# Second-layer weight sums taken in the attention loop, and splits of activations ordered later and joined in twos, in a fused attention and expert kernel

## The chip, the cores and the metric

The kernel runs on one core of a Trainium2 chip. The metric is the device time of one execution in microseconds. The engines have short names: PE is TensorE's matmuls and PEld its weight loads, DVE is VectorE, ACT is ScalarE, POOL is GpSimd, and SP issues most DMAs. PSUM has eight banks; every product of TensorE lands in one and has to be read out by DVE or ACT before the bank is used again.

## What is computed

Three layers follow each other: attention over keys and values that are averaged in eights, a mixture of experts in which every expert sees every token with a weight P from eight rounds of normalization, and a gated MLP. Cut to its core:

```python
# attention: q, k, v are (4, 8, 576, 64)
k_p = k.reshape(B, H, S // 8, 8, D).mean(axis=3)
v_p = v.reshape(B, H, S // 8, 8, D).mean(axis=3)
x = softmax(q @ k_p.T / sqrt(D)) @ v_p          # then laid out as (2304, 512)
# experts: w1 (8, 512, 1024), w2 (8, 1024, 512)
P = exp(x @ w_gate - max)
for _ in range(8):
    P /= P.sum(1, keepdims=True) + 1e-09
    P /= P.sum(0, keepdims=True) + 1e-09
    P *= N / E
out = sum(P[:, e:e+1] * (maximum(x @ w1[e], 0.0) @ w2[e]) for e in range(8))
# gated MLP: w_gate, w_val (512, 1536), w_out (1536, 512)
g = out @ w_gate
result = (g * sigmoid(g) * (out @ w_val)) @ w_out
```

## The kernel before

**Precision.** Every operand of a product is split into a high and a low part ("hi" and "lo", `split`): ACT copies the value to the rounded type (hi), and POOL or DVE subtracts hi from the value (lo). A product then is three matmuls (lines 114 to 116: hi·hi, hi·lo, lo·hi).

**Strassen products.** A 512-wide piece of a layer is worked as seven products M1 to M7 of half-size blocks instead of eight. Their operands are sums of blocks: on the weights' side `take_sums` (first layer, POOL, lines 695 to 698) and `row_sums` (second layer, DVE, lines 760 to 763), and on the activations' side a few sums too. The products of a piece share three PSUM banks, a, b and c; `part_sum` (line 985, ACT) copies an intermediate sum out of bank a, DVE adds it to what lies in another bank.

**Order.** Nothing is scheduled by a machine: each engine executes its instructions in the order in which the program issues them, and an instruction that waits holds up all that its engine has behind it. The author steers by queues in the Python code: `tasks` (work hung on a product's name), `late` (work to be issued at the next point, by `later()`), `side` (steps taken one at a time by `pump`), `do` (work for a point of a pair).

**Stages.** The attention loop (`for i in range(2, n_att)`, 20 row tiles) runs from about 50 to 183 us. One round i issues the query copy `qT` (line 271), scores, exponential (line 293), the multiplication by the reciprocal sum on POOL (line 303), the averages of values on POOL (line 244), and the stores of the result to `x_d`: hi from SP (line 477), lo added to it by a DMA that POOL issues (line 478). Between them `fill()` and `unit()` put matmuls of the first expert piece ("group 0", banks `hps` and `yps`), which keep TensorE busy. The PSUM pool `h` has two banks, shared by `qps`, `hps` and `gps`.

Pass 1 (about 224 to 726 us) works 30 `quad`s on the first 768 tokens: seven products, and between them six tiles `yps` of the second layer of the quad before (`second_tile`, lines 1054 to 1056, read out by DVE in line 1298 or 1300). The pool `y` has four banks. Meanwhile the quad prepares weights: first-layer sums, the splits of the w2 rows (`split_rows`), the row sums on DVE at M6, their split at M4 (ACT line 65, POOL line 66), and stores of all of these to DRAM (`w1s_d`, `w2s_d`). In the first quads the eight normalization rounds of P run too (lines 802 to 816).

Passes 2 and 3 (726 to 1645 us) read these sets back. Here `expert_quad`s run in 30 pairs; a pair's results are weighted by P (`whole`: lines 1354 and 1357), split (`split_h`: ACT line 1188, POOL or DVE line 1189) and combined (`sum_h`, POOL line 1201), and the second layer of the pair before is worked as seven `block`s (bank `mbs`, line 1245), one each after the points in `at_block`. Up to about 1470 us `conv` steps (ACT line 903, DVE lines 904 to 920) convert the weights of the last layer, one step a `pump`. The tail (1645 to 2113 us) is the gated MLP.

## Time and profile before

| what | value |
|---|---|
| three runs | 2111.4, 2116.02, 2122.97 us (median 2116.02) |
| the profiled execution | 2114.75 us |
| its span, first to last instruction | 2113.0 us |
| mean granted TensorE clock | 0.982 of full speed |
| busy share of the span: PE, DVE, POOL, ACT | 95%, 79%, 64%, 40% |
| TensorE not busy, 50 to 185 us | 5.2 us |
| TensorE not busy, 227.6 to 317 us (first quads) | 22.4 us |
| TensorE not busy, 317 to 725.8 us | 4.4 us |
| TensorE not busy, 725.8 to 763 us (pair 0) | 5.3 us |
| TensorE not busy, 763 to 1470 us (pairs with conversion) | 36.6 us |
| TensorE not busy, 1644.6 to 2113 us (tail) | 17.2 us |

The shares are averages over stages with different limits. What counts is, in each stage, how long TensorE stands or runs slowly and which engine's result it then waits for.

### The profile page before, as it was taken

The page shows a single profiled execution, that of the slowest core. Times are in us where ns is not written, and L with a number is a line of the kernel's source. Part 1 is how long each engine was busy: PE and PEld are TensorE (multiplying, and loading weights), DVE is VectorE, ACT ScalarE, POOL GpSimd, SP SyncE. Part 2 cuts the span into 40 slices and gives each one's busy share as a digit, 9 for nine tenths or more (in the row PEclk, how much of TensorE's full clock was granted, in tenths as well). Part 3 has the DMA queues.
Part 4 walks back from the last instruction along what each step waited for, and adds up shares of the span by engine and source line. Part 5 has one row for each costly group of instructions (what it writes and reads, how often), then busy time and mean ns, then how long its engine had stood idle before and what let it go on. Part 6 is the DMA issues. An engine that isn't in the chain of part 4 may idle for free.

```text
span 2113.0 us, 30988 instructions
## 1 busy us (share of the span) xinstructions
PE 2008.7 (95%) x11079; PEld 1891.9 (90%) x11079; DVE 1664.4 (79%) x2299; ACT 840.7 (40%) x1641; POOL 1361.4 (64%) x1117
## 2 busy tenths in 40 slices
PE   7999779999999989999999989999999899999999
PEld 7899668899999889999998989999999889899898
DVE  7774688888888868989887988988666867867776
ACT  3443324444444433333333422333333454544543
POOL 4444558888888467877776767877656546444432
PEclk8999889999999999999999999999999999999999
DMA  6463548888888788888888888888788654544442
GB/s 160 108 134 94 185 180 323 299 303 302 308 296 314 291 264 309 313 313 290 308 298 282 282 284 302 300 316 296 264 258 264 210 199 150 174 165 140 150 153 87
DMA packets 225754, 510.67 MB, mean 242 GB/s; under 512 B 35296, under 2 KB 119872, under 8 KB 219456
## 3 DMA queue, kind: packets, MB, share of 16 engines
q1 hardware_dynamic: 220704, 492.96, 67.9%
q0 software_dynamic: 4896, 15.73, 2.7%
q8 instruction: 88, 1.44, 0.3%
q14 instruction: 66, 0.54, 0.1%
HBM read 357.58 MB, written 151.04 MB: 241 GB/s over the span
## 4 chain that ended last, share of the span: by engine, by line
PE 69%; DVE 17%; DMA 7%; issue 3%; ACT 2%; POOL 2%; SPq 0%; ACTq 0%; DVEq 0%; POOLq 0%
PE aps L114 6%; PE aps L116 6%; PE aps L115 6%; PE yps L1054 5%; PE yps L1056 5%; PE yps L1055 5%; PE mbs L114 4%; PE mbs L115 4%; PE mbs L116 4%; PE cps L114 4%; PE cps L116 3%; PE cps L115 3%; DVE AC L1245 2%; DVE LR L1189 2%; DMA craw<-in_moe_w_val_dram 2%
## 5 line engine op out<-in xcount | busy, mean ns | idle before, releaser
L1201 POOL TENSOR_TENSOR LF<-LF 128x384 f32<-128x384 f32 x240 | 281.6, 1174 | 230.2 <-DVE LF L1357 136.6
L1188 ACT ACTIVATE LR<-LF 128x384 fp32r<-128x384 f32 x420 | 209.7, 522 | 373.9 <-DVE LF L1357 253.9
L985 ACT COPY LF<-aps 128x384 f32<-128x384 f32 x378 | 178.8, 473 | 401.5 <-PE aps L116 401.2
L1189 POOL TENSOR_TENSOR LR<-LF,LR 128x384 fp32r<-128x384 f32 x240 | 291.8, 1239 | 29.0 <-ACT LR L1188 29.0
L114 PE MATMUL mbs<-LR 128*128 128x384 f32 x840 | 285.1, 339 | 3.7 <-DVE AC L1245 3.7
L115 PE MATMUL mbs<-LR 128*128 128x384 f32 x840 | 284.0, 338 | 0.0
L116 PE MATMUL mbs<-LR 128*128 128x384 f32 x840 | 283.5, 338 | 0.0
L1054 PE MATMUL yps<-LR 128*128 128x512 f32 x576 | 229.3, 398 | 10.5 <-DVE AC L1300 6.3
L1245 DVE TENSOR_TENSOR AC<-mbs,AC 128x768 f32<-128x768 f32 x196 | 186.2, 950 | 67.2 <-PE mbs L116 66.9
L1056 PE MATMUL yps<-LR 128*128 128x512 f32 x576 | 228.0, 396 | 0.5 <-DVE LR L1498 0.5
L1055 PE MATMUL yps<-LR 128*128 128x512 f32 x576 | 227.6, 395 | 0.0
L734 POOL TENSOR_TENSOR LR<-praw,LR 128x512 fp32r<-128x512 f32 (+1 forms) x130 | 134.6, 1055 | 142.3 <-ACT LR L728 142.3
L734 POOL TENSOR_TENSOR LR<-sums,LR 128x1024 fp32r<-128x1024 f32 x65 | 159.5, 2454 | 60.7 <-ACT LR L728 60.7
L114 PEld LDWEIGHTS mbs<-LR 128*128 128x128 f32 x840 | 158.9, 189 | 5.5 <-DVE AC L1245 5.5
L115 PEld LDWEIGHTS mbs<-LR 128*128 128x128 f32 x840 | 159.0, 189 | 0.0
L116 PEld LDWEIGHTS mbs<-LR 128*128 128x128 f32 x840 | 158.8, 189 | 0.0
L1075 DVE SCALAR_TENSOR_TENSOR LR<-LF,LR 128x384 fp32r<-128x384 f32 x90 | 101.8, 1131 | 54.7 <-ACT LR L1074 54.7
L1189 DVE TENSOR_TENSOR LR<-LF,LR 128x384 fp32r<-128x384 f32 x180 | 136.8, 780 | 8.7 <-ACT LR L1188 8.7
L1357 DVE SCALAR_TENSOR_TENSOR LF<-LF,LR 128x384 f32<-128x384 f32 x180 | 135.6, 753 | 6.2
L1054 PEld LDWEIGHTS yps<-LR 128*128 128x128 f32 x576 | 110.1, 191 | 31.4 <-DVE AC L1300 8.5
L66 POOL TENSOR_TENSOR LR<-rraw,LR 128x512 fp32r<-128x512 f32 x72 | 114.0, 1603 | 30.4 <-ACT LR L65 29.1
L1056 PEld LDWEIGHTS yps<-LR 128*128 128x128 f32 x576 | 110.0, 191 | 25.2 <-DVE LR L1498 1.0
(284 smaller groups left out, 5662.8 us busy)
## 6 DMA issues: line engine op xcount, KB each, us to landing
LR<-w1s_d SPq DMA_DIRECT2D x210, 512.0 KB, 5.8
LR<-w2s_d SPq DMA_DIRECT2D x210, 512.0 KB, 5.3
w1s_d<-LR SPq DMA_DIRECT2D x29, 1792.0 KB, 8.5
w2s_d<-LR SPq DMA_DIRECT2D x30, 1024.0 KB, 4.2
w2s_d<-LR SPq DMA_DIRECT2D x90, 256.0 KB, 5.4
praw<-in_moe_w_dram SPq DMA_DIRECT2D x30, 512.0 KB, 6.0
rraw<-in_moe_w_dram SPq DMA_DIRECT2D x30, 512.0 KB, 5.0
LR<-rows_d POOLq DMA_DIRECT2D x12, 1024.0 KB, 7.2
```

Of the source, the lines that this page charges most:

```text
L114: nc.tensor.matmul(ps, lhsT=wh, rhs=ah, start=start, stop=False, skip_group_check=more)
L115: nc.tensor.matmul(ps, lhsT=wh, rhs=al, start=False, stop=False, skip_group_check=more)
L116: nc.tensor.matmul(ps, lhsT=wl, rhs=ah, start=False, stop=stop, skip_group_check=more)
L734: nc.gpsimd.tensor_tensor(out=lo, in0=src, in1=hi.bitcast(F32), op=ALU.subtract)
L985: nc.scalar.copy(out=t, in_=ps[:, :HB])
L1054: nc.tensor.matmul(ps, lhsT=hh[:, o:o + P], rhs=wh, start=j == 0, stop=False)
L1055: nc.tensor.matmul(ps, lhsT=hh[:, o:o + P], rhs=wl, start=False, stop=False)
L1056: nc.tensor.matmul(ps, lhsT=hl[:, o:o + P], rhs=wh, start=False, stop=j == 1)
L1188: nc.scalar.activation(out=hi, in_=src, func=AF.Copy)
L1189: f = lambda: eng.tensor_tensor(out=lo, in0=src, in1=hi.bitcast(F32), op=ALU.subtract)
L1201: nc.gpsimd.tensor_tensor(out=r(o), in0=r(a), in1=r(b), op=ALU.subtract)
L1245: nc.vector.tensor_tensor(out=acc_of(m), in0=ps[:, :, :HB], in1=acc_of(m), op=ALU.add)
```

## The change

**Early sums.** The row sums of the first 8 of 30 quads (`NEARLY`) are taken by a generator, `early_row_sums`, of which the attention loop runs four steps at the end of each round from i = 4 on. A set takes two rounds: load (SP), three sums (POOL), then the fourth sum (POOL), the hi copy (ACT), two halves of the lo part (POOL); the store is issued with the next load. For these eight quads pass 1 has no `row_sums` and no `split_row_sums` any more. In pass 1 the stores of the rows go from M7 to M3 and those of the row sums from M3 to M2 of the next quad.

**PSUM.** The pool `y` has three banks instead of four in pass 1, pair 0 and the tail, and c has two banks in turn there.

**Passes 2 and 3.** M4 now comes ahead of M3 in a quad. The weighing of the results 22 and 12 is one operation of 768 columns, several sums and splits are done two at a time, and they are issued at later points. The order of the blocks is now M1, M3, M2, M5, M7, M6, M4.

**Changes of pass.** The additions and stores of `combine` become single steps in `late`, or, after the last pass, in `side` during the tail; the fills of pair 0 are spread differently.

The diff, cut to its core:

```diff
+    def take_row_sums(eng, r, t):
+        a11, a12, a21, a22 = (r[:, k, c:c + 2 * P] for c in (0, 2 * P) for k in (0, 1))
+        for o, a, b, op in ((1, a21, a22, ALU.add), (2, t[:, 1], a11, ALU.subtract), (3, a11, a21, ALU.subtract),
+                            (0, a12, t[:, 2], ALU.subtract)):
+            yield lambda o=o, a=a, b=b, op=op: eng.tensor_tensor(out=t[:, o], in0=a, in1=b, op=op)
...
+    def early_row_sums():
+
+        t = AC[:, 6 * DM:8 * DM].rearrange("p (m f) -> p m f", m=4)
+        w = AC.bitcast(F32R)[:, 8 * DM:12 * DM].rearrange("p (m h f) -> p m h f", m=4, h=2)
+        for i in range(NEARLY):
+            r = rawp.tile([P, 2, DM], F32, tag="raw", name=f"early{i}")
+            nc.sync.dma_start(out=r, in_=rows[i].rearrange("(j p) d -> p j d", p=P))
+            yield
+            for f in take_row_sums(nc.gpsimd, r, t):
+                f()
+                yield
+            nc.scalar.activation(out=w[:, :, 0], in_=t, func=AF.Copy)
+            yield
+            for c in range(2):
+                m = slice(2 * c, 2 * c + 2)
+                nc.gpsimd.tensor_tensor(out=w[:, m, 1], in0=t[:, m], in1=w[:, m, 0].bitcast(F32), op=ALU.subtract)
+                yield
+            keep_row_sums(i, w)
...
             mask_values()
+            if i > 3:
+                for _ in range(4):
+                    next(early_sums, None)
...
-        pools["y"] = ps_open.enter_context(tc.tile_pool(name="ps_y2", bufs=4, **left))
+        pools["y"] = ps_open.enter_context(tc.tile_pool(name="ps_y2", bufs=3, **left))
+        banks_c = [ps_c, ps_open.enter_context(tc.tile_pool(name="ps_c2", bufs=1, **left))]
...
                 if expert:
+                    if n > NEARLY:
+                        at("M2", lambda: store_row_sums(n - 1))
                     at("M2", lambda: store_set(i))
-                    if n == 1:
-                        at("M2", lambda: split_row_sums(0))
-                        at("M5", lambda: store_row_sums(0))
-                    at("M6", lambda: row_sums(n))
-                    at("M4", lambda: split_row_sums(n))
-                    at("M3", lambda: store_row_sums(n))
+                    if n >= NEARLY:
+                        at("M6", lambda: row_sums(n))
+                        at("M4", lambda: split_row_sums(n))
                 at("M7", lambda: load_rows(n + 1))
-                at("M7", lambda: store_rows(n))
+                at("M3", lambda: store_rows(n))
...
             prod("M7")
             u3 = part_sum(banks["a"], "u3")
-            point("M7", lambda: whole("22", banks["c"], u3))
+            point("M7", lambda: csum("22", banks["c"], u3))
+            prod("M4")
+            point("M4", lambda: weigh("21", 1, banks["a"]))
             prod("M3")
-            point("M3", lambda: whole("12", banks["c"], u2))
-            prod("M4")
-            point("M4", lambda: whole("21", banks["a"], None))
+            point("M3", lambda: csum("12", banks["c"], u2), lambda: weigh("12", 2))
...
-            on(0, 0, lambda: split_h(0, "M1", r_of(0, "11")))
-            on(0, 2, lambda: split_h(0, "M3", r_of(0, "22"), V))
-            on(0, "M3", lambda: [sum_h(0, t) for t in ("T1", "T3", "T2")])
-            on(1, "M1", lambda: split_t(0, "T1"))
-            on(1, 3, lambda: split_h(1, "M1", r_of(1, "11")), lambda: split_t(0, "T2"))
-            on(1, 4, lambda: split_t(0, "T3"))
-            on(1, 5, lambda: split_h(0, "M2", r_of(0, "21"), V), lambda: split_h(1, "M3", r_of(1, "22"), V))
-            on(1, "M3", lambda: sum_h(0, "T4"), lambda: [sum_h(1, t) for t in ("T1", "T3", "T2")])
-            on(1, "M4", lambda: split_h(1, "M2", r_of(1, "21"), V))
-            on(1, 6, lambda: split_t(0, "T4"), lambda: sum_h(1, "T4"), lambda: split_t(1, "T1"))
+            on(0, 1, lambda: split_h(0, "M1", "11", 1, G))
+            on(0, "M3", lambda: sum_t13(0))
+            on(1, 3, lambda: split_h(0, "M3", "22", 2, V))
+            on(1, "M6", lambda: sum_t24(0))
+            on(1, 4, lambda: split_h(0, "M5", "11", 2, G), lambda: split_h(1, "M1", "11", 1, G))
+            on(1, "M3", lambda: sum_t13(1))
+            on(1, 6, lambda: split_h(1, "M3", "22", 2, V), lambda: split_h(0, "M6", "22", 2, V))
...
+            if j == NPR - 1:
+                rest.extend(combine(NPASS - 1, m))
+            elif last:
+                for f in combine(1 + j // (NQ // 2), m):
+                    late.append(f)
```

How the instructions stand on three engines, before and after. First ACT in round 7 of the attention loop; `e_110` holds the scores of tile 9, `kp` averaged keys, `AC` the buffer in which the early sums lie, `qT` the transposed queries, `hh` the hi part of group 0's activations, `aTh` that of the transposed attention weights. Before:

```order
L293 ACTIVATE e_110<-e_110 64x576
L220 COPY kp<-kp 128x5x64
L271 COPY qT<-qps 128x512
L135 ACTIVATE hh<-hps 128x256
L331 ACTIVATE aTh<-mps 128x5x128
```

After, with the line numbers of the changed program:

```order
L329 ACTIVATE e_110<-e_110 64x576
L256 COPY kp<-kp 128x5x64
L204 ACTIVATE AC<-AC 128x4x256
L307 COPY qT<-qps 128x512
L135 ACTIVATE hh<-hps 128x256
L367 ACTIVATE aTh<-mps 128x5x128
```

The copy of the early sums (L204) now stands between the key copy and the query copy. POOL in rounds 6 and 7: the multiplications of tiles 8 and 9 (`e_112`, `e_110`) and the averages of values (`kv`, `vp`). Before:

```order
L303 TENSOR_TENSOR e_112<-e_112,st 128x576
L244 TENSOR_TENSOR kv<-kv 128x256
L244 TENSOR_TENSOR kv<-kv 128x128
L244 TENSOR_TENSOR vp<-kv 128x64
L303 TENSOR_TENSOR e_110<-e_110,st 64x576
```

After:

```order
L339 TENSOR_TENSOR e_112<-e_112,st 128x576
L187 TENSOR_TENSOR AC<-early_920 128x256
L187 TENSOR_TENSOR AC<-AC,early_920 128x256
L187 TENSOR_TENSOR AC<-early_920 128x256
L280 TENSOR_TENSOR kv<-kv 128x256
L280 TENSOR_TENSOR kv<-kv 128x128
L280 TENSOR_TENSOR vp<-kv 128x64
L339 TENSOR_TENSOR e_110<-e_110,st 64x576
L187 TENSOR_TENSOR AC<-early_920,AC 128x256
L208 TENSOR_TENSOR AC<-AC 128x2x256 x2
```

Three sums of a set stand ahead of the averages, and the fourth, for which the copy on ACT waits, behind the multiplication. Last, DVE in the second half of a quad of passes 2 and 3, with steps of the conversion between: `cps` and `aps` are the banks c and a, `mbs` the bank of a second-layer block. Before:

```order
L1354 TENSOR_TENSOR LF<-cps,LF 128x384
L1357 SCALAR_TENSOR_TENSOR LF<-LF,LR 128x384
L908 TENSOR_SCALAR LF<-LF 128x512
L1245 TENSOR_TENSOR AC<-mbs,AC 128x768
L912 SCALAR_TENSOR_TENSOR LF<-craw,LF 128x512
L1189 TENSOR_TENSOR LR<-LF,LR 128x384
L1354 TENSOR_TENSOR LF<-cps,LF 128x384
L1357 SCALAR_TENSOR_TENSOR LF<-LF,LR 128x384
L1357 SCALAR_TENSOR_TENSOR LF<-aps,LR 128x384
L916 TENSOR_SCALAR LF<-LF 128x512
```

After:

```order
L1382 TENSOR_TENSOR LF<-cps,LF 128x384
L939 TENSOR_SCALAR LF<-LF 128x512
L1270 TENSOR_TENSOR AC<-mbs,AC 128x768
L943 SCALAR_TENSOR_TENSOR LF<-craw,LF 128x512
L1390 SCALAR_TENSOR_TENSOR LF<-aps,LR 128x384
L1382 TENSOR_TENSOR LF<-cps,LF 128x384
L1390 SCALAR_TENSOR_TENSOR LF<-LF,LR 128x768
L947 TENSOR_SCALAR LF<-LF 128x512
```

The weighing of 22 left its place behind the first sum and is joined with that of 12; the reading of bank a (21) now comes ahead of the second sum.

## Rows read from the trace of the kernel before

**Rows 1.** Busy time by stage, the attention loop; columns as the second line.

```profile
core 0: us, PE busy (x) PEld busy (x) DVE busy (x) ACT busy (x) POOL busy (x), PEclk, DMA share, GB/s
...
50.00:185.00 135.00, 129.78 (x974) 119.53 (x973) 90.17 (x150) 58.07 (x119) 52.58 (x70) 1.00 0.48 116
```

**Rows 2.** Waits of TensorE, 185 to 330 us: total us, times, longest.

```profile
PE yps L1054 <- DVE AC L1300: 4.7, 1, 4.7
PE sps L825 <- DVE pr L816: 4.4, 1, 4.4
...
PE yps L1054 <- DVE cs L812: 4.1, 1, 4.1
```

**Rows 3.** Waits of TensorE, 763 to 1470 us.

```profile
PE cps L114 <- DVE LF L1354: 22.3, 21, 2.3
PE aps L114 <- ACT LF L985: 15.0, 12, 4.1
```

**Rows 4.** Waits of ACT, 763 to 1470 us.

```profile
ACT LF L903 <- DMA craw<-in_moe_w_gate_dram: 24.4, 8, 5.2
```

**Rows 5.** Timeline of DVE, 249 to 256 us: start, us, then the instruction.

```profile
251.29 0.93 DVE L760 TENSOR_TENSOR LF<-rraw 128x256 f32<-128x256 f32 x1 [2.28 <-POOL LR L66]
...
254.73 0.15 DVE L812 TENSOR_SCALAR cs<-sps 128x8 f32<-128x8 f32 x1
```

**Rows 6.** Timeline of all engines, 540.5 to 545 us, a quad of pass 1.

```profile
541.05 0.39 PE L1054 MATMUL yps<-LR 128*128 128x512 f32 x1
...
543.77 0.34 PE L114 MATMUL aps<-T3h,LR 128*128 128x384 f32 x1
...
544.63 0.74 DVE L1300 SCALAR_TENSOR_TENSOR AC<-yps,pr,AC 128x512 f32<-128x512 f32 x1
...
544.81 0.39 PE L1054 MATMUL yps<-LR 128*128 128x512 f32 x1
```

**Rows 7.** Busy time in stretches at 1.2 GHz (clock 0.50); columns as in rows 1.

```profile
255.30:265.50 10.20, 7.50 (x19) 5.43 (x18) 9.36 (x21) 0.84 (x2) 3.77 (x3) 0.50 0.79 272
...
306.50:313.30 6.80, 4.84 (x11) 3.79 (x12) 6.26 (x10) 0.52 (x1) 0.96 (x1) 0.50 0.77 265
...
1081.40:1084.80 3.40, 3.40 (x13) 3.40 (x12) 2.27 (x5) 0.82 (x2) 0.00 (x0) 0.50 0.75 296
```

**Rows 8.** Groups by line and shape: xcount | busy, mean ns | idle before.

```profile
L65 ACT ACTIVATE LR<-LF 128x1024 fp32r<-128x1024 f32 x30 | 31.5, 1051 | 0.0
...
L698 POOL TENSOR_TENSOR sums<-praw,sums 128x256 f32<-128x256 f32 x30 | 27.1, 904 | 0.0
```

**Rows 9.** Timeline of all engines, 87.9 to 90.1 us, round 7.

```profile
87.94 0.69 ACT L293 ACTIVATE e<-e 64x576 f32<-64x576 f32 x1
...
88.88 0.58 ACT L271 COPY qT<-qps 128x512 f32<-128x512 f32 x1
...
89.59 0.36 PE L114 MATMUL hps<-xh,wh 128*128 128x256 f32 x1
...
90.01 1.15 POOL L303 TENSOR_TENSOR e<-e,st 64x576 f32<-64x576 f32 x1 [1.64 <-PE mps L329]
```

**Rows 10.** Timeline of POOL, 98 to 116 us, round 9.

```profile
111.53 1.24 POOL L478 DMA_DIRECT2D x_d<-xl  x1 [9.71 <-PE mps L279]
...
113.36 2.58 POOL L257 TENSOR_TENSOR vh<-vp_h,hmask 128x512 fp32r<-128x512 f32 x2
```

**Rows 11.** Timeline of TensorE, 105 to 114 us, round 9.

```profile
109.92 1.14 PE L279 MATMUL mps<-kbd,qT 128*128 128x144 f32 x8
```

**Rows 12.** Waits of ACT, 725 to 763 us, pair 0.

```profile
ACT LF L1133 <- DMA x_d<-LF: 9.4, 4, 5.1
```

**Rows 13.** Groups by line and shape, as in rows 8.

```profile
L1189 POOL TENSOR_TENSOR LR<-LF,LR 128x384 fp32r<-128x384 f32 x240 | 291.8, 1239 | 29.0 <-ACT LR L1188 29.0
...
L1189 DVE TENSOR_TENSOR LR<-LF,LR 128x384 fp32r<-128x384 f32 x180 | 136.8, 780 | 8.7 <-ACT LR L1188 8.7
...
L1354 DVE TENSOR_TENSOR LF<-cps,LF 128x384 f32<-128x384 f32 x120 | 66.1, 551 | 25.5 <-ACT LF L985 24.3 <-ACT LR L1188 0.8
...
L628 POOL TENSOR_TENSOR xq<-x,xq 128x768 f32<-128x768 f32 x6 | 11.4, 1904 | 0.1
```

More of the change, by code (lines that the diff above doesn't have):

```diff
@@ L175, in fused_kernel, with keep_row_sums @@
     w2s_d = dram.tile([P, NQ // 2, 7, 2, 2 * 2 * P], F32, name="w2s_d")
+    NEARLY = 8
+    quads, rows = [], []
+    for e in range(E):
+        for f0 in range(F // 2 if e == 0 else 0, F, 2 * P):
+            quads.append(w1[e, :, f0:f0 + 2 * P])
+            rows.append(w2[e, f0:f0 + 2 * P, :])
+    def take_row_sums(eng, r, t):
[3 more added lines that the diff above has]
+            yield lambda o=o, a=a, b=b, op=op: eng.tensor_tensor(out=t[:, o], in0=a, in1=b, op=op)
+    def keep_row_sums(i, w):
+        j, q = divmod(i, 2)
+        nc.sync.dma_start(out=w2s_d[:, j, 1:5, q], in_=w.bitcast(F32).rearrange("p m h f -> p m (h f)"))
+    def early_row_sums():
[15 more added lines that the diff above has]
+            keep_row_sums(i, w)
     ps_stack = ExitStack()
@@ L651, in first_x32 @@
             nc.gpsimd.tensor_tensor(out=x32[n], in0=xh32[sl], in1=xl32[sl], op=ALU.add)
-        quads, rows = [], []
-        for e in range(E):
-            for f0 in range(F // 2 if e == 0 else 0, F, 2 * P):
-                quads.append(w1[e, :, f0:f0 + 2 * P])
-                rows.append(w2[e, f0:f0 + 2 * P, :])
         NE = NPASS * NQ
@@ L1000, in new_c @@
         def new_c():
-            return ps_c.tile([P, 512], F32, tag="c", name="cps")
+            banks_c.append(banks_c.pop(0))
+            return banks_c[-1].tile([P, 512], F32, tag="c", name="cps")
         def quad(i, ys, tasks, sink):
@@ L1150, in load_unit1 @@
                                   in_=w1s_d[:, j, 2 * v:2 * v + 2])
-        ORDER = [(j, m) for j in range(NPR) for m in (BX if j < NPR - 1 else ("M1", "M3", "M2", "M5", "M6", "M7", "M4"))]
+        HX = ("M1", "M3", "M2", "M5", "M7", "M6", "M4")
+        RX = ("11", "12", "22", "21")
+        ORDER = [(j, m) for j in range(NPR) for m in HX]
         def block_set(v):
@@ L1184, in fused_kernel, with split_h @@
         GT = AC[:, 7 * TB:8 * TB].rearrange("p (c t) -> p c t", c=2)
-        def split_h(q, m, src, eng=nc.gpsimd):
-            hi, lo = h_of(q, m)
+        def split_h(q, m, name, n, eng):
+            hi, lo = (h_pair(q, m, n)[:, :, h] for h in (0, 1))
+            src = r_of(q, name, n)
+            if n == 1:
+                hi, lo = hi[:, 0], lo[:, 0]
             nc.scalar.activation(out=hi, in_=src, func=AF.Copy)
@@ L1245, in block @@
                 nc.vector.tensor_tensor(out=acc_of(m), in0=ps[:, :, :HB], in1=acc_of(m), op=ALU.add)
-            if last:
-                combine(1 + j // (NQ // 2), m)
+            if j == NPR - 1:
[3 more added lines that the diff above has]
+                    late.append(f)
         def group0_steps(p):
@@ L1346, in prod, with csum, weigh @@
                 product(banks[k], w[:, 0], w[:, 1], m, at)
-                if s % 2:
+                used.append(s // 2)
+                if used.count(s // 2) == 2:
                     load_unit1(s // 2 + 4)
-            def whole(name, ps, t):
-                r = r_of(q, name)
-                src = ps[:, :HB]
-                if t is not None:
-                    nc.vector.tensor_tensor(out=r, in0=src, in1=t, op=ALU.add)
-                    src = r
+            def csum(name, ps, t):
+                nc.vector.tensor_tensor(out=r_of(q, name), in0=ps[:, :HB], in1=t, op=ALU.add)
+            def weigh(name, n, src=None):
+                r = r_of(q, name, n)
                 h = int(name[1]) - 1
-                nc.vector.scalar_tensor_tensor(out=r, in0=src, scalar=0.0, in1=pb[:, h * HB:(h + 1) * HB],
+                w = pb[:, h * HB:(h + 1) * HB]
+                if n > 1:
+                    w = w.unsqueeze(1).to_broadcast([P, n, HB])
+                nc.vector.scalar_tensor_tensor(out=r, in0=r if src is None else src[:, :HB], scalar=0.0, in1=w,
                                                op0=ALU.max, op1=ALU.mult)
@@ L1381, in expert_quad @@
             prod("M2")
-            point("M2", lambda: whole("11", banks["b"], s1))
+            point("M2", lambda: csum("11", banks["b"], s1), lambda: weigh("11", 1))
             prod("M5")
@@ L1458, in fused_kernel @@
         assert not do and not side
+        side.extend(rest)
         ps_open.close()
[L1460 removed]
+        pools["y"] = ps_open.enter_context(tc.tile_pool(name="ps_y3", bufs=3, **left))
+        banks_c.append(ps_open.enter_context(tc.tile_pool(name="ps_c3", bufs=1, **left)))
         turn = count()
```

92 lines of the change are left out of this document (39 added, 53 removed).

## Prediction

> **What bounds the kernel now.** I read the view of stages first, then the waits of TensorE inside each stage, then single waits in order of time. TensorE sets the time: it is busy for 95% of the span, and where it runs without a gap one quad of pass 1 takes 15.5 us. So only a moment in which TensorE stands, or runs at half its clock, can be won or lost; work of the other engines counts where its lateness reaches TensorE. In the attention stage it hardly ever stands: 129.8 of 135 us are busy at full clock, while GpSimd (POOL) is used for 52.6 us [rows 1]. The worst places are the first quads of pass 1, with three long stalls [rows 2], and the pairs of passes 2 and 3 in which the weights of the last layer are converted [rows 3, 4]. The four row-sum operations of a quad stand on VectorE (DVE) in one piece, and what TensorE waits for is behind them [rows 5, 6].
>
> The profiled execution took 2114.75 us, 1.75 more than its span and 1.3 less than the median of the three runs, 2116.0. I sum against the profiled one and put the difference on the median.
>
> **Early sums, where they are taken away.** Eight of thirty quads lose 4 DVE, 1 ScalarE (ACT) and 2 POOL operations each. In quads 1 to 3 this is on the path. The wait of 4.1 us ends with L812, which follows four sums that run from 251.29 to 254.73, 3.4 us [rows 2, 5]; the waits of 4.4 and 4.7 have 3.1 and 4.1 us of sums ahead of what they wait for, read in the same way. So 10.6 us come back. After these stalls the granted clock fell to 1.2 GHz three times; TensorE was busy for 7.5 us in the first stretch and 4.8 in the last, 17.7 in all three, and half of that is lost: 8.9 [rows 7]. Some shorter stalls will remain, since DVE keeps the scaling of the router and the input splits there; I take 7. **Term: -18**, between -8 (stalls shrink, the clock stays) and -22 (no stall is left).
>
> **Early sums, where they are put.** Two rounds of the attention loop carry one set: three POOL sums in one, then the fourth sum, an ACT copy and two POOL differences in the next, then a store and a load on SP. POOL takes 0.90 us for such a sum and ACT 1.05 for such a copy [rows 8]. Both engines have room. The price lies in ACT's order: the copy stands directly ahead of the query copy (qT), and it waits for the fourth sum, which stands on POOL behind the multiplication of the round (L303). That one needs the exponential that ACT has only just made. Round 7 shows it: the exponential starts at 87.94; the multiplication ends at 91.16; the sum would end at 92.06, the copy at 93.11, and qT, which ran at 88.88, would be done near 93.5. TensorE used qT's PSUM bank again at 89.59 [rows 9]. That is 3.9 us; with the three sums of the round before, 2.7 us of POOL work against 1.64 us of idle time ahead of L303, it is 5.0. Where a round also has POOL's accumulating DMA into x_d and the values' masks ahead of the sum it is worse: in round 9 the masks end at 115.94, so the copy would end at 117.9 and qT at 118.3, while TensorE needed qT at 109.92: 8.4 us [rows 10, 11]. Worked out in this way for all eight rounds (5, 7, ... 19): 3.5, 5.0, 8.4, 3.2, 3.2, 3.4, 2.0, 6.4, together 35.1. Of the 5.2 us in which TensorE already stands in that stage some 3 fall into these stalls. **Term: +32**, from +10 (only what lies behind the x_d DMA stays) to +50 (the stores that now stand ahead of the next x_d store on SP push the DMA rounds by several us each). The loads and stores, 12 MB, lie beside other transfers.
>
> Clock after these stalls: today the stage runs at 2.4 GHz throughout [rows 1]. In passes 2 and 3 a stretch at 1.2 GHz that follows a stall lasts 3.4 us, in pass 1 6.8 to 10.2, half of which is lost [rows 7]. Eight times 3.4 us cost 14, eight times 6.8 cost 27, none of them 0. **Term: +15.**
>
> **One PSUM bank fewer for y (pass 1, pair 0, tail).** In a steady quad the first y tile is complete soon after the second starts, at 541.05, but it leaves its bank only behind the four sums, from 544.63 to 545.37; the fourth y tile starts at 544.81 [rows 6], in a bank of its own. With three banks it takes the first tile's, and has to wait until 545.37: 0.56 us, and about 0.05 for the signal. The 21 quads from the ninth on would all pay: 21 x 0.61 = 12.8. The eight quads without sums, pair 0 and the tail, where no sums stand ahead of that step, pay nothing. A second bank for the combined products (c) removes no wait that shows. **Term: +13**, from 0 (DVE frees the bank first) to +17 (where the quads' tiles sit closer).
>
> **Passes 2 and 3.** Two kinds of wait hold TensorE in the conversion pairs: for the sum on the bank c, 22.3 us in 21 waits, and for a copy from the bank a, 15.0 in 12 [rows 3]. With M4 ahead of M3, the six products of M4 now lie between the sum of 22 and the product that needs its bank; six such take 1.04 us (543.77 to 544.81 in [rows 6]). So each of the 21 waits (1.06 on average, 2.3 at the longest) loses up to 1.04: about 14 of 22.3. Of the 15.0, the ones behind ACT's conversion step, which itself waits up to 5.2 us for a load [rows 4], stay; splits issued later and in twos (14 to 8 on ACT in a pair) free perhaps 8. Four stretches of half clock, 3.4 us each, cost 7 there; I take 4 back. POOL's five merged operations save 5 x (2 x 1.24 - 1.90) = 2.9 us in a pair [rows 13]; that hides, since POOL's lateness reaches TensorE only through ACT's splits, counted above. **Term: -26**, from 0 to -44.
>
> **Spread changes of pass.** In pair 0 ACT waits 9.4 us for stores into x_d, 5.1 at the longest, ahead of a copy that TensorE needs [rows 12]; the fills are spread, and the combine steps of the later changes go one by one to free places and to the tail, beside its products. **Term: -10**, from 0 to -17 (the whole of those waits, and half as much again at the last change).
>
> Sum: -18 + 32 + 15 + 13 - 26 - 10 = +6. On the median that is **2122**.
>
> **A rule weighed against the rows.** POOL's split of 384 columns takes 1.24 us, one operation of 768 columns 1.90; DVE's split of 384, whose two inputs lie in SBUF, takes 0.78 on average, while its sum of the same width with one input in PSUM takes 0.55 [rows 13]. The Trainium skill, "SBUF — State Buffer" (section "Who interferes with whom"), says that a DVE instruction with two SBUF inputs and a GpSimd instruction that reads SBUF exclude each other for the whole instruction. By that rule the trace's 0.23 us are the mean price of meeting one, and a merged POOL operation makes it longer: the third rival.
>
> **The rivals.** (1) *Faster: ACT's wait does not last.* If POOL gets to the fourth sum before the multiplication is held up (it has 82 us to spare in the stage), only the rounds with the x_d DMA stall: 17 instead of 32, and with so few stalls the clock costs 3 instead of 15. Against it: the multiplication comes first in POOL's order, and its exponential comes late on ACT. For it: POOL's idle time. Time: 2122 - 15 - 12 = 2095, and 2080 if passes 2 and 3 give nearly all.
> (2) *Slower: the stalls of attention feed each other.* Place: POOL, between two sets. It decides as soon as POOL is late by more than its idle time in a round (1.64 us in round 7), for then each set starts late, and SP's store, which waits for it, holds the queue with the x_d stores. Price: +50 instead of +32, and the clock falls for 6.8 us each time, +27 instead of +15: 2122 + 30 = 2152.
> (3) *Slower: passes 2 and 3 give nothing.* A merged POOL operation holds DVE up for 0.66 us more than a plain one when they meet; if six DVE operations of a pair meet one, that is 4 us in a pair, and M4's 1.04 us of cover are used up. The -26 goes to zero: 2148. The edit then doesn't do what it says.
>
> **How the numbers follow.** Forecast as above 0.37; rival 1, 0.28; rival 2, 0.22; rival 3, 0.13. A measurement of this kernel tells apart about 0.5%, 10.6 us. The forecast's case lies around no change, rival 1 below it by more than that, rivals 2 and 3 above. So faster 0.28, same 0.37, slower 0.35. The range leaves out the outer ends of rivals 1 and 2: 2082 to 2151; the likeliest case alone would be 2106 to 2135.
>
> **What would show it.** Right: waits of TensorE for qT or an h bank in the rounds 5, 7, ... 19, ACT idle ahead of its 1024-wide copy on POOL, and granted clock under 1 between 70 and 200 us; a wait of 0.6 us for L1300 in each quad from the ninth on; no wait for L812 behind sums; waits on c down to about 8 us. Wrong: attention as long as before (then rival 1, and the time is under 2100), or waits on the banks c and a in passes 2 and 3 still near 37 us (rival 3).

## The result and the profile after

The changed kernel takes 2142.2 us (median of four runs, 2138.9 to 2147.0); the kernel before takes 2115.6. The ratio is 1.0124, with a 95% interval from 1.0089 to 1.0158: slower by 26.6 us. The forecast was 2122, within 2082 to 2151; the time lies near the upper end, above the 2106 to 2135 of the likeliest case. The difference is more than the 10.6 us that the prediction took as told apart, so it is the "slower" to which it gave 0.35.

The profiled execution of the changed kernel has a span of 2145.3 us, 32.3 more than before; that is 5.7 more than the medians differ by, for this execution is the longest of the four (2147.0). If a quad is counted from its first copy out of bank a, the stages of the two programs can be laid side by side:

| stage | before, us | after, us | difference |
|---|---|---|---|
| attention and group 0, up to the first quad | 227.6 | 281.0 | +53.4 |
| quads 0 to 7 | 152.8 | 127.0 | -25.8 |
| quads 8 to 28 | 326.9 | 344.5 | +17.6 |
| quad 29 | 18.5 | 15.7 | -2.8 |
| pair 0 | 37.2 | 33.5 | -3.7 |
| pairs with conversion (quads 32 to 76) | 706.1 | 703.6 | -2.5 |
| pairs without (77 to 88) | 175.5 | 175.5 | 0.0 |
| last quad and last blocks | 35.1 | 37.4 | +2.3 |
| rest of the tail | 433.3 | 427.1 | -6.2 |

One line of this table misleads. The copy that ends pair 0 is one that ACT makes late in both programs, and 14 matmuls change sides with it. Counted on TensorE, from the first product with T1 in quad 30 to the same product in quad 32, and from there to that of quad 77, the matmuls are the same but for one record. Before (columns as in the view below):

```profile
729.35:761.05 31.70, 27.12 (x146) 25.79 (x145) 13.53 (x22) 10.46 (x20) 9.24 (x9) 0.89 0.77 259
761.05:1472.00 710.95, 673.65 (x3775) 661.44 (x3775) 626.58 (x832) 242.81 (x497) 535.86 (x447) 0.99 0.86 299
```

After:

```profile
771.69:804.15 32.46, 27.43 (x145) 25.06 (x144) 19.86 (x27) 12.10 (x22) 11.91 (x9) 0.95 0.77 257
804.15:1508.20 704.05, 677.91 (x3775) 666.98 (x3775) 609.72 (x714) 216.20 (x358) 486.39 (x331) 0.98 0.86 301
```

So pair 0 gained nothing (31.7 and 32.5 us), and the pairs with conversion gained 6.9 us, not 2.5.

Here is the view of stages of the changed kernel, for five of them (us; then busy us and instructions of each engine, granted clock, DMA share, GB/s):

```profile
core 0: us, PE busy (x) PEld busy (x) DVE busy (x) ACT busy (x) POOL busy (x), PEclk, DMA share, GB/s
0.00:281.00 281.00, 222.63 (x1522) 203.45 (x1522) 146.66 (x249) 99.27 (x193) 144.21 (x172) 0.91 0.53 143
281.00:408.00 127.00, 120.59 (x589) 108.33 (x590) 91.82 (x157) 48.86 (x96) 80.12 (x68) 0.96 0.68 246
408.00:752.50 344.50, 332.83 (x1640) 295.40 (x1639) 271.93 (x359) 148.90 (x274) 280.04 (x210) 1.00 0.81 284
...
801.70:1505.30 703.60, 677.46 (x3768) 666.53 (x3767) 610.17 (x715) 215.37 (x358) 485.33 (x331) 0.98 0.86 301
...
1718.20:2145.30 427.10, 414.42 (x2154) 383.56 (x2152) 307.09 (x435) 207.07 (x401) 199.25 (x137) 1.00 0.47 157
```

TensorE executes as many matmuls in the first stage as before (1522 records in both), but is not busy for 58.4 us of it, against 18.4 before, and the same matmuls keep it busy for 13.4 us longer, at a granted clock of 0.91 instead of 0.97. In the attention loop the row of 50 to 185 us, to be read against [rows 1], shows 0.90 and 107 us busy:

```profile
50.00:185.00 135.00, 107.18 (x712) 97.44 (x713) 70.56 (x121) 49.34 (x97) 68.19 (x88) 0.90 0.52 141
```

Who waits there, and for what? First ACT's waits from 60 to 235 us, then those of POOL, then those of TensorE from 50 to 235 us (total us, times, longest):

```profile
ACT AC L204 <- POOL AC L187: 53.0, 8, 9.6
```

```profile
POOL AC L187 <- DMA early<-in_moe_w_dram: 19.4, 6, 6.6
```

```profile
PE hps L114 <- ACT qT L307: 20.7, 4, 7.1
PE gps L404 <- ACT lt L397: 7.2, 1, 7.2
PE mps L365 <- POOL e L339: 3.8, 1, 3.8
PE qps L304 <- ACT qT L307: 3.4, 1, 3.4
PE gps L392 <- ACT qT L307: 3.2, 1, 3.2
```

All eight copies of the early sums (L204) made ACT stand, 53.0 us in all, and TensorE then waited for what ACT had behind them. Round 7, which the prediction worked through in [rows 9], looks like this on ACT (85 to 100 us) and on POOL (90.5 to 101 us):

```profile
91.70 0.69 ACT L329 ACTIVATE e<-e 64x576 f32<-64x576 f32 x1
92.29 0.45 ACT L256 COPY kp<-kp 128x320 f32<-128x320 f32 x1
98.89 1.06 ACT L204 ACTIVATE AC<-AC 128x1024 fp32r<-128x1024 f32 x1 [6.16 <-POOL AC L187]
99.85 0.57 ACT L307 COPY qT<-qps 128x512 f32<-128x512 f32 x1
```

```profile
93.27 0.72 POOL L187 TENSOR_TENSOR AC<-early 128x256 f32<-128x256 f32 x1 [2.80 <-DMA early<-in_moe_w_dram]
...
94.75 0.72 POOL L187 TENSOR_TENSOR AC<-early 128x256 f32<-128x256 f32 x1
...
97.04 1.14 POOL L339 TENSOR_TENSOR e<-e,st 64x576 f32<-64x576 f32 x1
98.14 0.71 POOL L187 TENSOR_TENSOR AC<-early,AC 128x256 f32<-128x256 f32 x1
```

On TensorE (90 to 101 us) the next matmul into a bank of `hps` is

```profile
100.47 0.58 PE L114 MATMUL hps<-xh,wh 128*128 128x256 f32 x1 [6.88 <-ACT qT L307]
```

The chain is this: POOL stands for the load of the set (2.80 us), takes three sums, then the averages of values, then the multiplication L339, then the fourth sum; ACT, idle for 6.16 us, copies it and only then makes qT, for which TensorE has waited 6.88 us.

In pass 1 the read-out of a y tile, L1328, now holds TensorE once in each quad (444 to 752 us):

```profile
PE yps L1086 <- DVE AC L1328: 8.6, 19, 0.5
```

The view counts as idle only a part of the delay: in the quad at 549 us the product into the y tile starts 0.79 us after the one ahead of it instead of 0.17, 0.62 us late, of which 0.45 count, and the next one follows 0.34 us later instead of 0.23.

In passes 2 and 3 the waits of TensorE (first fence, 801.7 to 1505.3 us, to be read against [rows 3]) have changed places, and so have those of ACT (second fence, against [rows 4]):

```profile
PE aps L114 <- ACT LF L1016: 17.7, 11, 3.0
PE cps L114 <- DVE LF L1382: 5.0, 8, 1.6
```

```profile
ACT LR L1227 <- DVE LF L1390: 143.6, 44, 9.3
ACT LF L934 <- DMA craw<-in_moe_w_val_dram: 41.4, 12, 10.3
ACT LF L934 <- DMA craw<-in_moe_w_gate_dram: 39.7, 11, 5.2
ACT LF L934 <- DMA craw<-in_moe_w_out_dram: 38.9, 10, 9.6
```

The waits on bank c fell from 22.3 to 5.0 us. But ACT now stands 120.0 us ahead of the conversion's first step (L934) until its load has landed; before, the same three rows added up to 61.9. The rows of before, with those for the splits (L1188):

```profile
ACT LR L1188 <- DVE LF L1357: 204.8, 93, 5.8
ACT LR L1188 <- POOL LF L1201: 65.7, 72, 2.7
...
ACT LF L903 <- DMA craw<-in_moe_w_val_dram: 24.3, 8, 6.2
ACT LF L903 <- DMA craw<-in_moe_w_out_dram: 13.2, 7, 3.4
```

Behind L934 in ACT's order are the copies out of bank a, and TensorE's waits for these grew from 15.0 to 17.7 us. In order of time, nine of the eleven waits, 16.9 of the 17.7 us, come right behind a conversion step for whose load ACT stood. The longest, on ACT (1118 to 1120 us) and on TensorE:

```profile
1118.92 0.66 ACT L934 ACTIVATE LF<-craw 128x512 f32<-128x512 f32 x1 [6.75 <-DMA craw<-in_moe_w_out_dram]
1119.48 0.47 ACT L1016 COPY LF<-aps 128x384 f32<-128x384 f32 x1
```

```profile
1120.01 0.45 PE L114 MATMUL aps<-T3h,LR 128*128 128x384 f32 x1 [3.00 <-ACT LF L1016]
```

### The profile page after: what moved, and what is told of

Same layout as the page of the kernel before. It is cut to its first block, busy times and chain, and to the rows that moved or that the text cites. A ratio compares the mean times of both kernels' runs of the same rounds, so it can differ in the third digit from the quotient of the medians.

```text
span 2145.3 us, 30456 instructions
## 1 busy us (share of the span) xinstructions
PE 2020.7 (94%) x11079; PEld 1903.8 (89%) x11079; DVE 1599.8 (75%) x2119; ACT 806.2 (38%) x1461; POOL 1323.7 (62%) x1005
## 4 chain that ended last, share of the span: by engine, by line
PE 52%; DVE 22%; DMA 10%; issue 6%; POOL 5%; ACT 3%; SPq 1%; POOLq 0%; ACTq 0%; DVEq 0%
PE aps L114 5%; PE aps L116 5%; PE aps L115 5%; PE yps L1086 4%; PE yps L1088 4%; PE yps L1087 4%; PE mbs L114 4%; PE mbs L115 3%; PE mbs L116 3%; PE cps L114 3%; PE cps L116 2%; PE cps L115 2%; DVE LF L1390 2%; DVE LF L187 2%; DVE AC L1270 2%
## 5 line engine op out<-in xcount | busy, mean ns | idle before, releaser
L1228 POOL TENSOR_TENSOR LR<-LF,LR 128x768 fp32r<-128x768 f32 (+1 forms) x148 | 243.5, 1666 | 60.1 <-ACT LR L1227 56.7
L1227 ACT ACTIVATE LR<-LF 128x768 fp32r<-128x768 f32 (+1 forms) x240 | 174.7, 761 | 208.1 <-DVE LF L1390 180.1
L1239 POOL TENSOR_TENSOR LF<-LF 128x384 f32<-128x384 f32 x120 | 154.1, 1284 | 95.3 <-DVE LR L1228 90.6
L770 POOL TENSOR_TENSOR LR<-sums,LR 128x1024 fp32r<-128x1024 f32 x65 | 160.0, 2462 | 53.5 <-ACT LR L764 53.4
L1235 POOL TENSOR_TENSOR LF<-LF 128x768 f32<-128x768 f32 x60 | 117.2, 1954 | 122.5 <-DVE LF L1390 122.4
L1390 DVE SCALAR_TENSOR_TENSOR LF<-LF,LR 128x384 f32<-128x384 f32 x120 | 138.4, 1154 | 4.1
L1328 DVE SCALAR_TENSOR_TENSOR AC<-yps,pr,AC 128x512 f32<-128x512 f32 x168 | 121.0, 742 | 25.3 <-PE yps L1088 25.2
```

Of the source, the lines that this page charges most:

```text
L770: nc.gpsimd.tensor_tensor(out=lo, in0=src, in1=hi.bitcast(F32), op=ALU.subtract)
L1227: nc.scalar.activation(out=hi, in_=src, func=AF.Copy)
L1228: f = lambda: eng.tensor_tensor(out=lo, in0=src, in1=hi.bitcast(F32), op=ALU.subtract)
L1390: nc.vector.scalar_tensor_tensor(out=r, in0=r if src is None else src[:, :HB], scalar=0.0, in1=w, op0=ALU.max, op1=ALU.mult)
```

## The experiments

Five of the kernels below were executed once (2132.1, 2128.9, 2146.3, 2106.3 and 2052.0 us). From these it is the lengths of the stages, read inside the one execution, that carry the argument.

**Is it ACT's order in the attention loop, or POOL's load?** The first experiment executes the same instructions, dealt out differently (`load` issues the transfer of a set; four steps still run in a round, so the four sums now fill one and the rest the next):

```diff
+        r = load(0)
+        yield
         for i in range(NEARLY):
-            r = rawp.tile([P, 2, DM], F32, tag="raw", name=f"early{i}")
-            nc.sync.dma_start(out=r, in_=rows[i].rearrange("(j p) d -> p j d", p=P))
-            yield
             for f in take_row_sums(nc.gpsimd, r, t):
                 f()
                 yield
+            if i + 1 < NEARLY:
+                r = load(i + 1)
             nc.scalar.activation(out=w[:, :, 0], in_=t, func=AF.Copy)
...
             keep_row_sums(i, w)
+            yield
...
         early_sums = early_row_sums()
+        next(early_sums)
```

> The changed kernel with the early sums dealt out differently: a set's load is issued one round earlier, all four POOL sums stand in the first round, and ACT's copy and the two POOL differences in the second. The same instructions are executed. In the changed kernel the first quad of pass 1 begins 53 us later than before (281.0 instead of 227.6 us), and ACT stands 53.0 us ahead of eight copies, waiting for the fourth sum. Theory A (ACT's order: the copy waits for a sum that stands behind the round's multiplication, and all of ACT's work for TensorE queues behind it): the wait goes to under 8 us, the first quad begins at 230 to 245 us, and the whole takes 2095 to 2110. Theory B (POOL simply has too much to do in the loop, or the transfers are in the way): the first quad still begins after 265 us, and the whole stays above 2125.

It takes 2106.6 us: a ratio of 0.9962 to the kernel before (0.9949 to 0.9974), where the change itself has 1.0124. The first quad begins at 248.1 us, three us later than Theory A gave, and Theory B falls. ACT's wait for the fourth sum fell from 53.0 to 12.3 us, somewhat more than the 8 expected (ACT's waits, 50 to 250 us):

```profile
ACT AC L211 <- POOL AC L187: 12.3, 4, 4.8
```

Three of the four waits that are left, 12.0 us, sit in rounds in which POOL stands with its accumulating DMA first, as the prediction had it for [rows 10]; the copy is a round behind its sums, and even that doesn't always do.

**How much of it is the landing of the load?** Here only the load moves a round ahead, and all else stays where the change put it:

```diff
+            for k, f in enumerate(take_row_sums(nc.gpsimd, r, t)):
+                if k == 3:
+                    nxt = load(i + 1) if i + 1 < NEARLY else None
+                    yield
+                f()
+                yield
+            r = nxt
             nc.scalar.activation(out=w[:, :, 0], in_=t, func=AF.Copy)
```

> The changed kernel with only the load of a set issued one round earlier; the fourth sum, ACT's copy and the differences stay where the change put them. In the changed kernel POOL stands 19.4 us ahead of first sums, waiting for loads that were issued in the same round. Theory A (ACT's order): POOL's waits for loads vanish, but ACT still waits 30 us or more ahead of its eight copies, and the first quad begins at 260 to 275 us. Theory C (the loads' landing is what makes the sums late): ACT's wait falls under 15 us and the first quad begins before 245 us.

2132.1 us. POOL's waits for loads are gone, ACT still stands 43.7 us ahead of the copies, and the first quad begins at 269.8 us. Theory C falls. Of the 53.4 us that the attention stage lost, 11.2 came from the landing of the loads; another 21.7 came back by taking the copy away from its sum (to 248.1), and 20.5 are what eight sets cost in this loop even so. Each of these parts is a difference of single executions: where the code up to the first quad is the same, its beginning differs by 2.1 us (225.5 and 227.6 in two executions of the kernel before, 245.9 and 248.1 in two with the first experiment's edit) and by up to 4.6 (278.8, 278.8, 281.0 and 283.3 in four with the change's).

**The fourth y bank.** In pass 1 and pair 0 alone:

```diff
-        pools["y"] = ps_open.enter_context(tc.tile_pool(name="ps_y2", bufs=3, **left))
-        banks_c = [ps_c, ps_open.enter_context(tc.tile_pool(name="ps_c2", bufs=1, **left))]
+        pools["y"] = ps_open.enter_context(tc.tile_pool(name="ps_y2", bufs=4, **left))
+        banks_c = [ps_c]
```

> The changed kernel with four y banks and one c bank again in pass 1 and pair 0; the tail keeps three and two. In the changed kernel quads 10 to 28 take 16.2 us instead of 15.5, with 11.7 us of waits for the read-out of a y tile. If the fourth bank is what they lack, these quads take 15.5 us and that wait is under 2 us: 21 quads x 0.7 = 15 us, and 2 to 4 more in quads 8 and 9, so 2122 to 2128 for the whole. If the second c bank is worth something in pass 1, other waits come instead and the quads stay above 15.8 us.

2128.9 us, and the quads 8 to 28 take 326.5 us instead of 344.5, as before the change (326.9); quads 10 to 28 are at 15.50 us each and no wait of TensorE for L1328 is left there. So the bank was lacking, for 18.0 us; with four y banks the quads run without a gap on one c bank, and a second had nothing left to give in pass 1.

**The banks of the tail.**

```diff
-        pools["y"] = ps_open.enter_context(tc.tile_pool(name="ps_y3", bufs=3, **left))
-        banks_c.append(ps_open.enter_context(tc.tile_pool(name="ps_c3", bufs=1, **left)))
+        pools["y"] = ps_open.enter_context(tc.tile_pool(name="ps_y3", bufs=4, **left))
```

> The changed kernel with four y banks and one c bank again in the tail alone. In the changed kernel the tail from its second pair of quads on takes 427.1 us instead of 433.3, 0.35 us less in each pair of a gate and a value quad, which the prediction had put at nothing. If the second c bank is the cause, the pairs take 23.2 us again and the whole is about 6 us longer, near 2148. If the steps of the last change of pass or anything else in the stage is the cause, the pairs stay at 22.85 us and the whole at 2142.

2146.3 us; most pairs of gate and value quads take 23.2 us again, and the rest of the tail 434.5 instead of 427.1. So the same exchange of a bank that costs 18 us in pass 1 gives time in the tail, where no four sums stand ahead of the read-out of y: 7.4 us between these two executions, and some five by all eleven profiled ones (426.9 to 429.0 us in the eight with three y banks and two of c, 432.0 to 434.5 in the three with four and one).

The traces show which wait it is. In each of the 36 quads of that stage, the first product into bank c (T1) starts 0.17 us after the product ahead of it where c has two banks, and 0.17 to 1.99 us where it has one; in sum that is 8.9 us. In the group of these products, first with two banks (1760 to 2040 us of the changed kernel), then with one (1765 to 2050 us of this experiment), the delay shows as 4.0 us of idle time and 1.8 us of longer products:

```profile
L114 PE MATMUL cps<-T1h,LR 128*128 128x384 f32 x48 | 16.1, 336 | 0.0
```

```profile
L114 PE MATMUL cps<-T1h,LR 128*128 128x384 f32 x48 | 17.9, 373 | 4.0 <-DVE LF L1525 3.3 <-DVE LF L1504 0.6
```

**Where the gain of passes 2 and 3 went.** Two empty steps are added to each half of the conversion, behind the load of the next half:

```diff
                     yield from [c[0], stored, c[1], c[2], begin if j == 0 else n, c[3], c[4], loads[2 * i + j + 1],
-                                n, out_sums if j == 1 else n, n]
+                                n, out_sums if j == 1 else n, n, n, n]
```

> The changed kernel with two empty steps after each half of the weight conversion, so that a half's load is issued six steps ahead of ACT's first step on it instead of four; the conversion ends some 130 us later, in pairs that so far have none. In the changed kernel ACT stands 120 us ahead of 33 such steps, waiting for loads, and TensorE waits 17.7 us for copies out of bank a in the pairs with conversion. Theory D (what is left of the waits in passes 2 and 3 is ACT's wait for these loads, which holds up the copies behind it): ACT's waits for loads fall below 50 us, TensorE's waits in that stage from 30 to under 15 us, and passes 2 and 3 take 12 to 25 us less. Theory E (merged POOL operations hold DVE up): the waits are spread over more pairs, their sum stays at 25 us or more, and the whole stays within 6 us.

2106.3 us: 36 less than the change, a good deal more than the 12 to 25 expected. ACT's waits for the loads fell to 25.9 us, the stage from 703.6 to 666.0 us, and TensorE is not busy for 6.5 us of it (26.1 in the change, 36.6 before). The view of stages has now, for 799 to 1465 us:

```profile
799.00:1465.00 666.00, 659.46 (x3765) 655.95 (x3765) 592.59 (x689) 211.93 (x354) 467.81 (x317) 1.00 0.88 311
```

Of the 37.6 us that the stage lost, 19.6 are less standing, which is within the expectation. The other 18.0 are less time for the matmuls themselves, and these the expectation had left out: in the change, this stage has seven stretches at 1.2 GHz, 27 us in all (the kernel before has four, 13.7 us); with the loads out of the way it has none, but for the one with which it begins in both. Theory D holds, and Theory E falls.

The edit does one thing more than to give the loads time: it thins the conversion out. Five of its 36 steps on ACT now fall into the pairs behind the stage, which take as long as in the change all the same (175.4 us in both, from the first product with T1 in quad 77 to that in quad 89). No run gives the loads time and leaves the density as it was. That it is the loads is told by the stalls themselves: of the eleven waits on bank a in the change, nine stood behind a late load, and one of 0.4 us is left here.

Does the new order of products and splits then do anything? The same two empty steps in the kernel before tell:

> The kernel before with the two empty steps after each half of the weight conversion, and nothing of the change. Its pairs with conversion take 706.1 us, the changed ones 703.6, and the changed ones with the empty steps 666.0. Theory D (the change does remove the waits on bank c, 22 us, but the waits for the loads took their place): here ACT's waits for loads fall from 62 to under 25 us, the waits on bank c stay near 20 us, and the stage takes 682 to 694 us, the whole 2090 to 2102. Theory F (the loads alone were the matter and the new order of products and splits is worth nothing): the stage takes 670 us or less here too, the whole under 2082.

2095.7 us, a ratio of 0.9913 (0.9891 to 0.9935). ACT's waits for loads are 2.6 us in all, and still TensorE waits (760 to 1448 us):

```profile
PE cps L114 <- DVE LF L1354: 17.6, 15, 2.8
PE aps L114 <- ACT LF L985: 4.5, 8, 1.2
```

The stage takes 687.6 us. So the pairs gain 18.5 us from the spacing alone, 2.5 from the change alone, and 40.1 from both; counted between the same products on TensorE (711.0 us before, 692.2, 704.1 and 666.9), it is 18.8, 6.9 and 44.1. With the loads out of the way, the new order of products and splits is worth 21.6 us by the first count and 25.3 by the second, close to the 26 that were forecast; with the loads as they are it is worth 2.5 or 6.9. Theory F falls.

**All three at once.** The early sums a round ahead, four y banks in pass 1 and the spaced conversion, together:

> The changed kernel with all three edits: early sums a round ahead of their copy, four y banks and one c bank in pass 1, the conversion spaced. If the three causes are apart from each other, their differences add: 2142 - 36 (sums) - 13 (banks) - 36 (spacing) = 2057, within 2049 to 2066, clearly faster than before. If they share waits, it stays above 2070.

2059.9 us, a ratio of 0.9742 (0.9721 to 0.9763): 82 us less than the change, where the three gains add up to 85 (36, 13 and 36). The causes hardly share a wait.

**Fewer sets.** Eight sets cost 20.5 us in the attention loop even when dealt out well, and only quads 1 to 3 had long stalls:

```diff
-    NEARLY = 8
+    NEARLY = 4
...
-                for _ in range(4):
+                for _ in range(2):
                     next(early_sums, None)
```

> As the kernel with the three edits, but four early sets instead of eight, two steps a round instead of four, so that a set takes four rounds. Only quads 1 to 3 had long stalls from their row sums; sets 4 to 7 saved 1.4 us in pass 1. Eight sets a round ahead still make the first quad begin 20 us later than in the kernel before. If that price goes with the number of sets and with POOL's load, the first quad begins at 232 to 240 us and the whole takes 8 to 15 us less than with eight sets, 2042 to 2050. If the price is one of the loop's start or end, it stays within 4 us.

2051.2 us, a ratio of 0.9704 (0.9681 to 0.9727): 8.7 us less than with eight sets, at the near end of the 8 to 15 expected; the runs of the two, 2048.2 to 2055.9 and 2057.9 to 2061.3 us, don't overlap. The first quad begins at 235.4 us, 10.5 earlier, so the price goes with the sets; as their number and the steps in a round were halved together, the run doesn't tell one from the other. This is the fastest version, 62 us under the kernel before in the same runs (2113.2).

**Quad 29.** The wait of 2.8 us for the first weights of pass 2 is gone in the change, which nobody had forecast. A guess was the place of the row stores ahead of that load on SP:

```diff
-                at("M3", lambda: store_rows(n))
+                at("M7", lambda: store_rows(n))
```

> The kernel with the three edits and four early sets, with the stores of the split rows back at M7, where the kernel before has them. In the kernel before, the last quad of pass 1 takes 18.5 us, with one wait of 2.8 us for the load of the first weights of pass 2, which SP issues behind three such stores; in the changed kernel it takes 15.7 and in the mended ones 15.5 us. If the place of the stores is the cause, the last quad takes 17.5 to 18.5 us again; if it is another part of the change (the row-sum store that moved to the next quad), it stays at 15.5.

2052.0 us, and quad 29 stays at 15.5 us. So the place of these stores is not it. The traces show another difference: before, the load of the weights P for pass 2 is issued 2.3 us into quad 29, ahead of the first load of expert weights, which follows 4.8 us into the quad; in the change and in this run P's load is issued in quad 28, and the first expert weights follow 2.8 us into quad 29. That this is the cause was not tried and stays open.

## Why the prediction was nearly right, and where it was wrong

The time lay in the range, and the forecast of 2122 was 20 us too low. That the range held is in part luck: attention, the y bank, passes 2 and 3 and the changes of pass came out 43 us dearer than their terms, and the early sums, quad 29 and the tail gave back 17 of it. Without these 17 the time would have been about 2159, outside the range (an estimate from the rows below). By terms, from the table of stages (in brackets the count between the same products):

| term | predicted | measured |
|---|---|---|
| early sums taken away (quads 0 to 7) | -18 | -25.8 |
| waits and clock in attention | +32 and +15 | +40.0 not busy, +13.4 at the low clock |
| one y bank fewer | +13 | +17.6 |
| passes 2 and 3 | -26 | -2.5 (-6.9) |
| spread changes of pass | -10 | -1.4 (+3.1) |
| quad 29, tail | 0 | -2.8 and -6.2 |

**Attention: right in place, mechanism and nearly in size.** The place (ACT's copy ahead of qT), the chain (multiplication, fourth sum, copy) and the clock behind the stalls are what the trace and the two experiments show. Round 7 was put at 5.0 us of delay and gave 6.9 of wait on TensorE, though the sums took 0.72 us each there and not 0.90. What was missed is the load: the text let the loads "lie beside other transfers", and did not see that three of the sums follow their load within the same round, for which POOL stood 19.4 us (2.80 in round 7). Eight stretches at 1.2 GHz came with the stalls, 41 us in all; half of that would be 20, and 13.4 were paid, since TensorE was busy for only 31.2 us of them. The first rival fell, and the second came true in part: the waits of ACT are longer in later rounds (7.2, 6.6, 8.6 and 7.5 us in four of the last five) than the terms for these rounds (3.2, 3.4, 2.0 and 6.4).

**Early sums taken away: right, and mis-sized.** The bound -22 was too tight. The three stalls went altogether, and not only the part of them that the sums had been: TensorE stands 16.8 us less where 10.6 were worked out. It is busy for 9.0 us less where 7 were taken, for the three stretches at half clock behind these stalls went too. Quads 6 and 7 fell to 15.5 us as well.

**The y bank: right.** Each of the 19 steady quads grew by 0.72 us where 0.61 was worked out (0.62 for the late first product, and 0.11 for the one behind it); quads 8 and 9, in which the tiles sit closer, lost 3.7 together. Taking the bank back returned the whole. The sentence that in the tail nothing changes was wrong by 6.2 us, in the other direction: the second c bank, priced at nothing for want of a wait that shows, takes away the delay of the first product into c (most often about 0.1 us, and as much again at the product behind it), and is worth a third of a us in most pairs there.

**Passes 2 and 3: the step that failed.** The waits on c went as predicted (22.3 to 5.0; about 14 of 22.3 were forecast to go, 17 did). The failed step is the sentence on the 15.0 us: that those behind ACT's conversion step "stay" and the others free 8. They did not stay; they grew. Put in order of time, about 8.8 of the 15.0 us before come behind a conversion step that waited for its load, and 6.1 behind splits. In the change 16.9 of 17.7 come behind such a step: the part behind splits went nearly whole, and the part behind loads doubled. In the kernel before, ACT spent 270 us of the stage ahead of splits (waiting for DVE and POOL) and 62 ahead of the loads; in the change, 147 and 120. The loads themselves land no later (median 4.9 to 6.0 us from issue to landing before, by the matrix that is loaded, and 4.4 to 5.4 in the change). So ACT, freed from waits for its splits, arrives at the conversion step earlier than its load. Between the same products TensorE stands 11.2 us less, but is busy for 4.3 us longer, with seven stretches at 1.2 GHz instead of four: 6.9 us gained where 26 were forecast. The third rival had nearly the right outcome (the -26 goes to zero) by the wrong cause: the merged POOL operations do lengthen DVE's, but the spaced conversion runs at nearly full rate with all of them in place. The weighing by P before, and then the groups of the changed kernel, against [rows 13]:

```profile
L1357 DVE SCALAR_TENSOR_TENSOR LF<-LF,LR 128x384 f32<-128x384 f32 x180 | 135.6, 753 | 6.2
```

```profile
L1228 POOL TENSOR_TENSOR LR<-LF,LR 128x768 fp32r<-128x768 f32 x88 | 173.8, 1975 | 53.6 <-ACT LR L1227 50.2 <-PE mbs L116 3.4
...
L1390 DVE SCALAR_TENSOR_TENSOR LF<-LF,LR 128x768 f32<-128x768 f32 x60 | 71.3, 1189 | 2.1
L1390 DVE SCALAR_TENSOR_TENSOR LF<-LF,LR 128x384 f32<-128x384 f32 x60 | 67.1, 1119 | 2.1
```

The weighing of 384 columns that is left is that of 11. Before, it took 0.857 us on average (the sixty of 11 alone, among the 180 of L1357), and now it takes 1.119. This fits what the Trainium skill, "SBUF — State Buffer" (section "Who interferes with whom"), says of DVE instructions with two SBUF inputs beside GpSimd's: the POOL operations that they meet grew from 1.24 to 1.98 us. But the merged weighing gives most of it back: all weighings from SBUF together take DVE 138.4 us, and took 135.6 before.

**Changes of pass: they gave nothing.** The 3.7 us of pair 0 in the table are matmuls that changed sides; between the same products it takes 0.8 us more. TensorE stands there once for 4.4 us in the change, as it did once for 4.6 before, now behind a copy (L1164) for which ACT waits up to 6.2 us for a store into x_d. The step that failed is that spreading the fills ends ACT's waits for these stores: they went from 9.4 to 7.6 us. The last quad took 2.3 us more.

## What to carry to other kernels

A step that is put into a loop because "its engines have room" costs what its slowest operand makes the next engine wait: look at what stands behind it in that engine's order, and put the consumer a full round behind the producer, and the load a round ahead of both. When one wait of an engine that executes in order is taken away, look up which wait it meets next (here loads of 0.5 MB, for which ACT stood 62 us in all before and 120 after) and move that too, or the gain is only exchanged. And price a bank of PSUM from the read-out that frees it, separately in each stage: the same exchange cost 18 us in one and gave some five in the other.

## What the runs showed of the hardware

The eight long stalls of TensorE in the attention loop (3.0 to 7.2 us) each came with a stretch at half the granted clock, of 3.4 to 10.2 us. At the five shorter stalls it began 0.3 to 0.9 us after TensorE had started again, at the three of about 7 us while it still stood. Three of these stretches, the first three, in the view of stages of the changed kernel (the column behind POOL is the granted clock):

```profile
76.80:80.20 3.40, 3.40 (x16) 3.06 (x14) 1.40 (x3) 0.72 (x2) 3.24 (x5) 0.50 0.00 0
97.20:104.00 6.80, 3.53 (x16) 3.38 (x16) 1.39 (x3) 2.80 (x5) 5.48 (x7) 0.50 0.14 44
128.00:138.20 10.20, 7.14 (x33) 6.73 (x34) 4.87 (x9) 4.79 (x10) 6.24 (x8) 0.50 0.66 164
```

In the attention loop 40.0 us more of standing cost 13.4 us more of matmul time in this way. In the conversion stage 11.2 us less of standing came with 4.3 us more, though the single waits did not grow: 33 of 1.13 us on average and 4.1 at the longest before, 26 of 0.99 and 3.0 after. Nor does the length of a single wait settle it: in the change one of 1.66 us on bank a (ended at 1462.5 us) was followed by a stretch at half clock, in the kernel before one of 2.17 us on bank c (ended at 1246.5 us) was not. So what a wait costs in clock has to be read from the granted clock behind it, not from the sum of the waits.
